# v prepared and loaded one block earlier, per-pair sums in another PSUM tile, squares on GpSimd, uneven block distances

## The chip, the cores and the metric

The kernel runs on one core of a Trainium2 chip. A core has a matrix engine (TensorE, PE in the profile) that writes to PSUM, three engines for element-wise work (VectorE as DVE, ScalarE as ACT, GpSimd as POOL), a queue engine that issues transfers (SyncE as SP), and 16 DMA engines. Each engine takes its own instructions in order; semaphores tie them together. The metric is the device time of one execution in microseconds, and lower is better.

## The reference

The program is attention with a sigmoid in place of a softmax, and a two-layer network behind it. Eight batches of 448 tokens, twelve heads of width 64, a model width of 768 and a hidden width of 2048:

```python
def _attn_ref(q, k, v):                      # (8, 12, 448, 64)
    S = q.shape[2]
    scale = 1.0 / np.sqrt(q.shape[-1])
    scores = scale * np.matmul(q, k.transpose(0, 1, 3, 2)) - np.log(S)
    attn = 1.0 / (1.0 + np.exp(-scores))
    return np.matmul(attn, v).astype(np.float32)

def _moe_ref(x, w_in, w_out):                # (3584, 768), (768, 2048), (2048, 768)
    h = x @ w_in
    g = h - np.tanh(h)
    return (g @ w_out).astype(np.float32)
```

## The kernel before

**Precision.** Most products are taken in float16 with each operand split into a high and a low half, three matmuls for one (high by high, high by low, low by high). A power-of-two scale goes with each split; it comes from sums of squares, which are summed over partitions by a small matmul against ones (`pbn` for q, k and v of a pair of heads, `nm` for x of a batch). The weights arrive in HBM as float64 and are converted on the chip during the first batch (`rawo` is a piece of `w_out` as it comes in, `stb` its converted form, `wl` the matmul over its squares).

**Stages.** Batch 0 takes its attention alone (`attention32`, in float32), while `w_in` is loaded and converted. After that the kernel alternates for each batch between `moe1` (x by `w_in`, 288 matmuls, PSUM tiles `ph`) and `moe2` (g by `w_out`, three groups of 128 tokens with 96 matmuls each into the two PSUM tiles of tag `mm`, and a last 64 tokens as `por`). The attention of the next batch is put into `moe2` in blocks. A group of tokens is counted in 16 steps of six `po` matmuls; the step numbers at which a block is put in are the tables `BLOCKS0` (batch 0), `BLOCKS1` (batch 1) and `BLOCKS` (later ones). A group ends at steps 16, 32 and 48: there ACT copies one half of its sum out of PSUM (L905, `o`), DVE the other (L906). The next group needs the same two PSUM tiles.

**Blocks.** `stream` takes two pairs of heads (128 columns each), g and h = g + 1, in four blocks, here called A, B, C and D. Each computes score tiles `sc` on PE, the sigmoid `a` of them on ACT (L394) and its two halves `ahl` (high on ACT L400, low on DVE L401).

- A: scores of g, chunks 0 and 1; then the products with v that are still owed (`do_av`), which closes the pair h before: ACT copies its result out as x (L430), squares it (`x2`, L439), and POOL adds the squares up (L448). Then the sums of squares of v for the next pairs (`norm_v`, two `sqn<-vn` on ACT, L317).
- B: scores of g, chunk 2 and the shared rest; sums of squares of k and q of g + 3. At steps 16, 32 and 48.
- C: the scales of g + 2 and g + 3 (`pbn` on PE, `tn` on ACT L330, small DVE instructions), scores of h, all products with v for g (closes g, with x and its square), the two halves `w` of k and q of g + 2, each of which goes through a transposing DMA to become K and Q.
- D: scores of h, chunk 2, k and q of g + 3 in the same way, and before the change the halves of v (`prep_v`, L369 and L370, `vhl`) of g + 2 and g + 3, and behind them the loads of v for g + 4 and g + 5 (`load_v`, into the two buffers `vn` that `prep_v` has just read).

In steady batches a batch starts with D at step 8, then A 12, B 16, C 20, D 24, A 28, B 32, C 36, D 40, A 44, B 48, C 52. `batch_scales` (`nm`) follows the last A by 3 steps.

**Order.** PE, ACT, DVE and POOL follow the order in which the program is written. SP's order, all loads and transposing DMAs, is made by the framework's scheduler. In batch 1 (whose attention runs in `moe2` of batch 0) q by k is split but v stays in float32: `early` is true there, so the products with v are spread over all four blocks and `pbn` uses a tile of the score tag `sc` (two buffers); later it uses the tag `av`.

Of the kernel before, what the change touches and what calls it, by code (L numbers as in the profile page):

```python
# [10 lines left out]
F32 = mybir.dt.float32  # L11
# [3 lines left out]
AF = mybir.ActivationFunctionType  # L15
ALU = mybir.AluOpType
# [3 lines left out]
P = 128  # L20
# [14 lines left out]
class Builder:  # L35
# [4 lines left out]
    SPLIT = 16, 0.78  # L40
    CONV = 0.95

    BLOCKS = (8, 12, 16, 20, 24, 28, 32, 36, 40, 44, 48, 52)
    TAIL = (1, 2, 3, 4, 5)
    ALONE = 9
    BLOCKS0 = (2, 5, 8, 12, 16, 20, 24, 31, 38)
    BLOCKS1 = (4, 7, 10, 13, 16, 20, 24, 28, 32, 36, 40, 44, 48, 52)

    TP = 8
    SHIFT = 4  # L50
# [268 lines left out]
    def scales(self, ss, where):  # L319


        nc = self.nc
        n = ss.shape[1] // 2
        if where == "sc":
            pb = self.ps.tile([P, 2, 512], F32, name="pbn", tag="sc", bufs=2)[:, 0, : 2 * n]
        else:
            pb = self.ps.tile([P, 512], F32, name="pbn", tag=where, bufs=1)[:, : 2 * n]
        nc.tensor.matmul(pb, self.onesf, ss, start=True, stop=True)
        t = self.sm.tile([P, 3, 2], F32, name="tn")
        nc.scalar.activation(  # L330
            t[:, :n].rearrange("p n i -> p (n i)"), pb, AF.Relu, bias=self.tiny, scale=2.1
        )
        u = self.sm.tile([P, 3], F32, name="un")
        nc.vector.tensor_tensor(u[:, :n], t[:, :n, 0], t[:, :n, 1], op=ALU.max)
        y = self.pow2(u[:, :n], n, "n")
        i = self.sm.tile([P, 3], F32, name="in")
        nc.vector.tensor_scalar(i[:, :n], y, 2.0**49, None, op0=ALU.mult)
        s = self.sm.tile([P, 3], F32, name="sn", bufs=3)
        nc.vector.reciprocal(s[:, :n], i[:, :n])
        r = self.sm.tile([P, 2], F32, name="rn", bufs=3)  # L340
        nc.vector.scalar_tensor_tensor(
            r[:, 0:1], i[:, 0:1], 1.0 / math.sqrt(D), i[:, 1:2], op0=ALU.mult, op1=ALU.mult
        )
        if n == 3:
            nc.vector.tensor_scalar(r[:, 1:2], y[:, 2:3], 2.0**49 / A_SCALE, None, op0=ALU.mult)
        return s, r
# [87 lines left out]
    def add_squares(self, j, x):  # L434

        nc = self.nc
        last = j == self.NP - 1
        x2 = self.xp.tile([P, self.S], BF16 if last else F32, name="x2", tag="x2", bufs=2)
        nc.scalar.activation(x2, x, AF.Square)  # L439
        if j == 0:  # L440
            self.x2 = x2
        elif last:
            self.x2b = self.x2, x2
        else:
            out = self.x2
            if j == self.NP - 2:
                out = self.xp.tile([P, self.S], BF16, name="x2b", tag="x2b", bufs=1)
            nc.gpsimd.tensor_tensor(out, self.x2, x2, op=ALU.add)  # L448
            self.x2 = out

    def stream(self):

        NP = self.NP
        G = (self.B - 1) * NP
        at = lambda g: (1 + g // NP, g % NP)
        splits = lambda g: at(g)[0] >= self.AV32
        qk, vn, sc, K, Q, vv, accs = {}, {}, {}, {}, {}, {}, {}  # L460

        def load(g):
            if g < G and g not in qk:
                qk[g] = self.load_qk(*at(g))

        def load_v(g):
            if g < G and splits(g):
                vn[g] = self.load_v(*at(g), self.nat, "vn", 2)

        def sums(g):  # L470
            ss = self.sums[g // 2 % 2]
            return ss if splits(g) else ss[:, :4]

        def norms(g):
            if g < G:
                for n, t in enumerate(qk[g]):
                    self.norm(t, sums(g)[:, 2 * n + g % 2 : 2 * n + g % 2 + 1])

        def norm_v(g):
            if g in vn:  # L480
                self.norm(vn[g], sums(g)[:, 4 + g % 2 : 5 + g % 2])

        def scales(g, where):
            if g < G:
                sc[g] = sc[g + 1] = self.scales(sums(g), where)

        def parts_k(g):
            if g < G:
                K[g] = self.parts(qk[g][0], sc[g][0][:, 0:1], "K", not splits(g) and g not in (2, 3))

        def parts_q(g):
            if g < G:
                Q[g] = self.parts(qk[g][1], sc[g][0][:, 1:2], "Q", True)
                qk.pop(g)

        def prep_v(g):
            if g >= G:
                return
            if splits(g):
                vv[g] = self.prep_v(vn.pop(g), sc[g][0])  # L500
            else:
                vv[g] = self.load_v(*at(g), self.att, "vhl", 3)[:, None]

        load(0)
        load(1)
        yield 0, False
        norms(0)
        norms(1)
        yield 0, False
        scales(0, "tr")  # L510
        parts_k(0)
        yield 450, False
        parts_q(0)
        load(2)
        yield 450, False
        parts_k(1)
        yield 450, False
        parts_q(1)
        load(3)
        yield 450, False  # L520
        norms(2)
        yield 0, False
        todo = []

        def open_acc(g):
            tag = "tr" if g % 2 else "av"
            accs[g] = self.ps.tile([P, 512], F32, name="acc", tag=tag, bufs=1)
            if g % NP == 0:
                self.xs = []

        def close_acc(g):
            iv = sc[g][1][:, 1:2] if splits(g) else None
            self.xs.append(self.evac_x(g % NP, accs.pop(g), iv))
            if g % 2:
                vv.pop(g - 1)
                vv.pop(g)
            for d in (sc, K, Q):
                d.pop(g)

        def do_av():  # L540
            for g, c, A in todo:
                odd = g % 2
                if c == QT:
                    open_acc(g + 1)
                    self.av([accs[g], accs[g + 1]], vv[g], A, c, odd)
                    close_acc(g)
                    continue
                if c == 0 and not odd:
                    open_acc(g)
                self.av([accs[g]], vv[g], A, c, odd)  # L550
                if c == QT - 1 and odd:
                    close_acc(g)
            todo.clear()

        def units(g, cs, between=lambda: None):

            pss = []
            for c in cs:
                n = 2 if c == QT else 1
                pss.append(self.scores([K[g + i] for i in range(n)], [Q[g + i] for i in range(n)], c))  # L560
            aa = [self.weigh(pss[0], sc[g][1][:, 0:1])]
            between()
            aa += [self.weigh(ps, sc[g][1][:, 0:1]) for ps in pss[1:]]
            return aa

        def keep(g, cs, aa):
            if splits(g):
                aa = [self.split_a(a) for a in aa]
            todo.extend((g, c, a) for c, a in zip(cs, aa))

        for g in range(0, G, 2):
            h = g + 1
            early = not splits(g)

            aa = units(g, (0, 1))
            do_av()
            if g == 0:
                prep_v(0)
                prep_v(1)
            keep(g, (0, 1), aa)  # L580
            load(g + 3)
            norm_v(g + 2)
            norm_v(g + 3)
            yield 2750, True

            aa = units(g, (2, QT))
            if early:
                do_av()
            norms(g + 3)
            keep(g, (2, QT), aa)  # L590
            yield 2750, True

            scales(g + 2, "sc" if early else "av")
            aa = units(h, (0, 1), lambda: parts_k(g + 2))
            do_av()
            keep(h, (0, 1), aa)
            parts_q(g + 2)
            load(g + 4)
            yield 2750, True

            aa = units(h, (2,), lambda: parts_k(g + 3))
            if early:
                do_av()
            keep(h, (2,), aa)
            parts_q(g + 3)
            prep_v(g + 2)
            prep_v(g + 3)
            load_v(g + 4)
            load_v(g + 5)
            norms(g + 4)  # L610
            yield 2750, True
        do_av()
        yield 1150, True
# [349 lines left out]
    def first(self, rest):  # L963
# [16 lines left out]
        next(rest)  # L980
        assert n + len(self.BLOCKS0) + len(self.BLOCKS1) == 4 * self.NP + len(self.BLOCKS) - self.ALONE
        split = self.split_w_in()
# [85 lines left out]
```

## Time and profile before

Three runs took 1281.15, 1287.76 and 1290.39 us. The profiled execution:

| | |
|---|---|
| median of three runs | 1287.76 us |
| profiled execution, its own time | 1281.98 us |
| its span | 1279.7 us |
| PE busy | 1190.1 us, 93% of the span |
| DVE, ACT, POOL busy | 908.4, 902.2, 37.9 us |
| one `moe1` (590.5 to 645.2 us) | 54.7 us, PE busy in all of it |
| `moe2` of batch 0 (153.5 to 282 us) | 128.5 us, PE busy 100.8 |
| `moe2` of batch 2 (496 to 590.5 us) | 94.5 us, PE busy 86.6 |

The page counts a matmul from its issue to its modelled end, and they overlap; 24 `po` matmuls take 4.07 us at the full clock, so 0.17 us each. What counts is where PE is idle, and the clock it is granted: 512 ns of idle time at the end of a group of tokens, with nothing between, is what the last batch shows; the batches with attention in them show more. In a row of the timeline the first two numbers are start and length in us, "xN" is a number of equal instructions merged into a row, and the bracket at its end says how long the engine had stood idle and which instruction ended that. A row of the waits reads: who, for whom, us in total, times, longest.

### The profile page before, as it was taken

The page shows a single profiled execution, that of the slowest core. Times are in us where ns is not written, and L with a number is a line of the kernel's source. Part 1 is how long each engine was busy: PE and PEld are TensorE (multiplying, and loading weights), DVE is VectorE, ACT ScalarE, POOL GpSimd, SP SyncE. Part 2 cuts the span into 40 slices and gives each one's busy share as a digit, 9 for nine tenths or more (in the row PEclk, how much of TensorE's full clock was granted, in tenths as well). Part 3 has the DMA queues.
Part 4 walks back from the last instruction along what each step waited for, and adds up shares of the span by engine and source line. Part 5 has one row for each costly group of instructions (what it writes and reads, how often), then busy time and mean ns, then how long its engine had stood idle before and what let it go on. Part 6 is the DMA issues. An engine that isn't in the chain of part 4 may idle for free.

```text
span 1279.7 us, 19703 instructions
## 1 busy us (share of the span) xinstructions
PE 1190.1 (93%) x7633; PEld 618.1 (48%) x7633; DVE 908.4 (71%) x1376; ACT 902.2 (70%) x1262; POOL 37.9 (3%) x38
## 2 busy tenths in 40 slices
PE   9899877699989999989999999999998999999998
PEld 3244323255445555445544555445554555455555
DVE  5899976678946689457975779556984689646940
ACT  6867785767877588766877768776877768763830
POOL 0100000000000000100000000000000000000000
PEclk9999999799999999999999999999999999999999
DMA  9963367120054400542024310353015410310000
GB/s 248 262 177 93 66 169 178 44 58 3 1 92 97 93 10 14 102 92 55 1 56 85 85 36 1 75 114 73 1 37 104 85 36 1 64 35 19 1 13 32
DMA packets 225678, 89.77 MB, mean 70 GB/s; under 512 B 213936, under 2 KB 215728, under 8 KB 225584
## 3 DMA queue, kind: packets, MB, share of 16 engines
q1 hardware_dynamic: 224656, 88.28, 30.5%
q8 instruction: 60, 0.98, 0.3%
q10 hardware_dynamic: 928, 0.23, 0.1%
q14 instruction: 34, 0.28, 0.1%
HBM read 58.20 MB, written 11.01 MB: 54 GB/s over the span
## 4 chain that ended last, share of the span: by engine, by line
PE 55%; DVE 13%; ACT 13%; DMA 9%; issue 6%; SPq 4%; DVEq 0%; ACTq 0%
PE ph L761 29%; PE po L876 12%; PE por L914 5%; PE acc L414 5%; DMA qn<-q 3%; PE sc L383 3%; ACT a L394 3%; DMA Q<-w 2%; SPq L298 2%; DVE ahl L401 2%; DMA rawo<-moe_w_out 1%; ACT sqn L317 1%; DVE m L835 1%; ACT ahl L400 1%; DVE m L849 1%
## 5 line engine op out<-in xcount | busy, mean ns | idle before, releaser
L876 PE MATMUL po<-wo,g 128*128 128x384 f16 x2304 | 402.6, 332 | 30.7 <-ACT o L905 28.8
L761 PE MATMUL ph<-xhl,wi 128*128 128x448 f16 x2016 | 382.6, 352 | 0.0
L876 PEld LDWEIGHTS <-g 128*128 128x128 f16 x2304 | 223.6, 99 | 212.7 <-issue 75.9
L761 PEld LDWEIGHTS <-wi 128*128 128x128 f16 x2016 | 196.7, 98 | 185.0 <-issue 2.1
L401 DVE SCALAR_TENSOR_TENSOR ahl<-a,ahl 128x896 f16<-128x896 f32 x126 | 137.7, 1127 | 178.9 <-ACT ahl L400 178.9
L394 ACT ACTIVATE a<-sc,nls,rn 128x896 f32<-128x896 f32 x147 | 154.2, 1089 | 24.7 <-PE sc L383 20.8
L831 ACT ACTIVATE u<-ph,ih 128x896 f32<-128x896 f32 x64 | 64.4, 1006 | 90.6 <-PE ph L761 85.9
L383 PE MATMUL sc<-Q,K 64*128 64x448 f16 x1008 | 104.3, 361 | 21.0 <-ACT tn L330 8.8
L400 ACT ACTIVATE ahl<-a 128x896 f16<-128x896 f32 x126 | 113.1, 939 | 0.6
L835 DVE SCALAR_TENSOR_TENSOR m<-ph,ihk,u 128x896 f32<-128x896 f32 x64 | 73.4, 1147 | 39.7 <-ACT th L833 39.4
L745 ACT ACTIVATE g<-m,Sg 128x896 f16<-128x896 f32 x64 | 66.6, 1041 | 39.2 <-DVE m L849 33.7
L414 PE MATMUL acc<-ahl,vhl 128*64 128x448 f16 (+1 forms) x864 | 82.1, 360 | 1.1 <-ACT tn L330 1.1
L849 DVE COPY_PREDICATED m<-u,th 128x896 f32<-128x896 uint32 x64 | 77.3, 1207 | 7.3 <-ACT u L831 0.5
L746 DVE SCALAR_TENSOR_TENSOR g<-m,Sg,g 128x896 f16<-128x896 f32 x64 | 73.4, 1147 | 6.8 <-ACT g L745 6.8
L846 DVE SCALAR_TENSOR_TENSOR m<-q,m 128x896 f32<-128x896 f32 x64 | 69.9, 1093 | 11.6 <-ACT q L845 3.9
L383 PEld LDWEIGHTS <-K 64*128 64x128 f16 x1008 | 36.9, 98 | 80.9 <-issue 58.8
L791 PE MATMUL ph<-x,wi 128*128 128x448 f32 x192 | 75.1, 540 | 0.2 <-DVE x L426 0.2
L836 DVE SCALAR_TENSOR_TENSOR th<-ph,ih,th 128x896 f32<-128x896 f32 x64 | 73.3, 1145 | 0.0
L848 ACT ACTIVATE u<-u,b 128x896 f32<-128x896 f32 x64 | 66.7, 1043 | 7.3 <-DVE m L835 5.4
L914 PE MATMUL por<-wo,g 128*64 128x384 f16 x768 | 64.9, 327 | 6.0 <-ACT o L905 6.0
L842 DVE SCALAR_TENSOR_TENSOR m<-q,m 128x896 f32<-128x896 f32 x64 | 69.6, 1088 | 0.0
L841 ACT ACTIVATE q<-u,b 128x896 f32<-128x896 f32 x64 | 65.8, 1029 | 0.0
(132 smaller groups left out, 1134.9 us busy)
## 6 DMA issues: line engine op xcount, KB each, us to landing
raw<-moe_w_in SPq DMA_DIRECT2D x24, 512.0 KB, 5.3
rawo<-moe_w_out SPq DMA_DIRECT2D x32, 384.0 KB, 4.1
kn<-k SPq DMA_DIRECT2D x96, 112.0 KB, 3.0
qn<-q SPq DMA_DIRECT2D x94, 112.0 KB, 3.0
vn<-v SPq DMA_DIRECT2D x96, 96.0 KB, 2.7
out<-o SPq DMA_DIRECT2D x21, 384.0 KB, 2.3
vn<-v SPq DMA_DIRECT2D x48, 32.0 KB, 2.5
out<-orem SPq DMA_DIRECT2D x16, 96.0 KB, 2.2
```

The source lines that it names most:

```text
L383: self.nc.tensor.matmul(ps[i * m : (i + 1) * m, h, : self.S], K[i][r, w, c * P : c * P + m], Q[i][r, x, :], start=(n == 0), stop=(n == len ...
L394: self.nc.scalar.activation(a[:, 0], ps[:, :, : self.S], AF.Sigmoid, bias=self.nls, scale=scale)
L400: nc.scalar.activation(A[:, 0], a[:, 0], AF.Copy, scale=A_SCALE)
L401: nc.vector.scalar_tensor_tensor(A[:, 1], a[:, 0], A_SCALE, A[:, 0], op0=ALU.mult, op1=ALU.subtract)
L414: self.nc.tensor.matmul(acc[i][h * D : (h + 1) * D, : self.S], v[k, w, 2 * QT + h if half else h * QT + c], A[k, x, h], start=(n == 0 and ...
L746: nc.vector.scalar_tensor_tensor(g[:, 1], m, Sg, g[:, 0], op0=ALU.mult, op1=ALU.subtract)
L761: nc.tensor.matmul(ph[:, e, :S], self.wi[:, c * self.NB + k, part, e * P : (e + 1) * P], xhl[c][:, x, :], start=(i == 0), stop=(i == 3 * s ...
L791: nc.tensor.matmul(ph[:, e, :S], self.where("in", c)[:, f * P : (f + 1) * P], xs[c], start=(c == 0), stop=(c == self.NC - 1),)
L835: V.scalar_tensor_tensor(m, ps, ihk, u, op0=ALU.mult, op1=ALU.mult)
L849: V.copy_predicated(m, u.bitcast(U32), th)
L876: nc.tensor.matmul(po[i][:, :H], gs[f // 2][:, x, f % 2, tk * P : (tk + 1) * P], self.wo[:, i * self.NF + f, w], start=(f == 0 and n == 0) ...
L914: nc.tensor.matmul(po[e * D : (e + 1) * D, :H], gs[f // 2][:, x, f % 2, nm:S], self.wo[:, e * self.NF + f, w], start=(f == 0 and n == 0), ...
```

## The change

Five edits go together. `prep_v` and `load_v` move from block D to block C, so the halves of v and the next loads of v stand one block sooner. `pbn` of the early pairs leaves the score tiles: it uses `mm` for g = 0 and `av` after that, and `early` now holds for g = 0 alone, so that the products with v of g = 2 and g = 4 are taken in A and C only. The squares of x go from ACT to POOL, but for the first and the last of a batch. Blocks at steps 12, 28 and 44 come at 11, 27 and 43 (all of them A); and `nm`, which hangs on the last, comes a step sooner too.

```diff
-    BLOCKS = (8, 12, 16, 20, 24, 28, 32, 36, 40, 44, 48, 52)
+    BLOCKS = (8, 11, 16, 20, 24, 27, 32, 36, 40, 43, 48, 52)
-    BLOCKS1 = (4, 7, 10, 13, 16, 20, 24, 28, 32, 36, 40, 44, 48, 52)
+    BLOCKS1 = (4, 7, 10, 13, 16, 20, 24, 27, 32, 36, 40, 43, 48, 52)
...
-        if where == "sc":
-            pb = self.ps.tile([P, 2, 512], F32, name="pbn", tag="sc", bufs=2)[:, 0, : 2 * n]
-        else:
-            pb = self.ps.tile([P, 512], F32, name="pbn", tag=where, bufs=1)[:, : 2 * n]
+        pb = self.ps.tile([P, 512], F32, name="pbn", tag=where, bufs=2 if where == "mm" else 1)[:, : 2 * n]
...
-        nc.scalar.activation(x2, x, AF.Square)
+        if last or j == 0:
+            nc.scalar.activation(x2, x, AF.Square)
+        else:
+            nc.gpsimd.tensor_tensor(x2, x, x, op=ALU.mult)
...
-            early = not splits(g)
+            early = g == 0
...
-            scales(g + 2, "sc" if early else "av")
+            scales(g + 2, "mm" if early else "av")
             aa = units(h, (0, 1), lambda: parts_k(g + 2))
             do_av()
+            prep_v(g + 2)
             keep(h, (0, 1), aa)
             parts_q(g + 2)
+            prep_v(g + 3)
             load(g + 4)
+            load_v(g + 4)
+            load_v(g + 5)
             yield 2750, True
...
             parts_q(g + 3)
-            prep_v(g + 2)
-            prep_v(g + 3)
-            load_v(g + 4)
-            load_v(g + 5)
             norms(g + 4)
```

What it does to the order is shown at three places. Line numbers behind L324 are lower by 3 in the changed kernel (L370 becomes L367, L401 becomes L398, L359 becomes L356).

The first is blocks C and D of a pair in `moe2` of batch 1, on DVE. In the names `w` is the pair of halves of k (`kn`) or q (`qn`), `sn` the scales, `vhl` those of v. Before:

```order
L357 SCALAR_TENSOR_TENSOR w<-kn,sn,w 112x512
L401 SCALAR_TENSOR_TENSOR ahl<-a_3092,ahl 128x896
L401 SCALAR_TENSOR_TENSOR ahl<-a_3099,ahl 128x896
L357 SCALAR_TENSOR_TENSOR w<-qn,sn,w 112x512
L356 TENSOR_SCALAR w<-kn,sn 112x512
L357 SCALAR_TENSOR_TENSOR w<-kn,sn,w 112x512
L401 SCALAR_TENSOR_TENSOR ahl<-a_3179,ahl 128x896
L357 SCALAR_TENSOR_TENSOR w<-qn,sn,w 112x512
L369 TENSOR_SCALAR vhl<-vn,sn 128x512
L370 SCALAR_TENSOR_TENSOR vhl<-vn,sn,vhl 128x512
L369 TENSOR_SCALAR vhl<-vn,sn 128x384
L370 SCALAR_TENSOR_TENSOR vhl<-vn,sn,vhl 128x384
```

The same place after the change:

```order
L354 SCALAR_TENSOR_TENSOR w<-kn,sn,w 112x512
L366 TENSOR_SCALAR vhl<-vn,sn 128x512
L367 SCALAR_TENSOR_TENSOR vhl<-vn,sn,vhl 128x512
L398 SCALAR_TENSOR_TENSOR ahl<-a_3092,ahl 128x896
L398 SCALAR_TENSOR_TENSOR ahl<-a_3099,ahl 128x896
L354 SCALAR_TENSOR_TENSOR w<-qn,sn,w 112x512
L366 TENSOR_SCALAR vhl<-vn,sn 128x384
L367 SCALAR_TENSOR_TENSOR vhl<-vn,sn,vhl 128x384
L353 TENSOR_SCALAR w<-kn,sn 112x512
L354 SCALAR_TENSOR_TENSOR w<-kn,sn,w 112x512
L398 SCALAR_TENSOR_TENSOR ahl<-a_3193,ahl 128x896
L354 SCALAR_TENSOR_TENSOR w<-qn,sn,w 112x512
```

The first v of the pair now stands ahead of C's two `ahl`, the second behind C's half of q; block D is four instructions shorter.

SP in `moe2` of batch 1, the pair whose block C stands at step 20 (K_3403 and Q_3453 are of g + 2, the next K and Q of g + 3). Before:

```order
L359 DMA_TRANSPOSE K_3403<-w_3400 128x8x112
L287 DMA kn_3455<-k 112x4x64 x2
L359 DMA_TRANSPOSE Q_3453<-w_3450 128x8x112
L287 DMA qn_3458<-q 112x4x64 x2
L359 DMA_TRANSPOSE K_3497<-w_3494 128x8x112
L287 DMA kn_3596<-k 112x4x64 x2
L359 DMA_TRANSPOSE Q_3505<-w_3502 128x8x112
L287 DMA qn_3599<-q 112x4x64
L298 DMA vn_3513<-v 128x3x64 x2
L302 DMA vn_3513<-v 64x2x64 x2
L298 DMA vn_3518<-v 128x3x64 x2
L287 DMA qn_3599<-q 112x4x64
```

The same place after the change:

```order
L356 DMA_TRANSPOSE K_3403<-w_3400 128x8x112
L287 DMA kn_3461<-k 112x4x64 x2
L298 DMA vn_3467<-v 128x3x64 x2
L302 DMA vn_3467<-v 64x2x64 x2
L356 DMA_TRANSPOSE Q_3456<-w_3453 128x8x112
L287 DMA qn_3464<-q 112x4x64 x2
L298 DMA vn_3472<-v 128x3x64 x2
L356 DMA_TRANSPOSE K_3511<-w_3508 128x8x112
L287 DMA kn_3590<-k 112x4x64
L356 DMA_TRANSPOSE Q_3519<-w_3516 128x8x112
L287 DMA kn_3590<-k 112x4x64
L287 DMA qn_3593<-q 112x4x64 x2
```

The six loads of v stood behind the last Q of the pair; four of them now stand ahead of the first Q, two ahead of the second K, and none is left in front of the next pair's q.

SP again, in `moe2` of batch 0, around the last pieces of `w_out` (`rawo`). Before:

```order
L359 DMA_TRANSPOSE Q_1658<-w_1655 128x8x112
L287 DMA qn_1663<-q 112x4x64 x2
L131 DMA rawo_1693<-moe_w_out 128x384
L131 DMA rawo_1707<-moe_w_out 128x384
L131 DMA rawo_1721<-moe_w_out 128x384
L298 DMA vn_1751<-v 128x3x64 x2
L131 DMA rawo_1778<-moe_w_out 128x384
L359 DMA_TRANSPOSE K_1735<-w_1732 128x8x112
L359 DMA_TRANSPOSE Q_1744<-w_1741 128x8x112
L131 DMA rawo_1792<-moe_w_out 128x384
```

The same place after the change:

```order
L356 DMA_TRANSPOSE Q_1663<-w_1660 128x8x112
L287 DMA kn_1668<-k 112x4x64 x2
L287 DMA qn_1671<-q 112x4x64 x2
L131 DMA rawo_1709<-moe_w_out 128x384
L131 DMA rawo_1723<-moe_w_out 128x384
L131 DMA rawo_1737<-moe_w_out 128x384
L131 DMA rawo_1774<-moe_w_out 128x384
L131 DMA rawo_1788<-moe_w_out 128x384
L356 DMA_TRANSPOSE K_1751<-w_1748 128x8x112
L356 DMA_TRANSPOSE Q_1756<-w_1753 128x8x112
```

The last piece of `w_out` stood behind the K and Q of block D, and now stands ahead of them; a load of k came ahead of the first of the five pieces.

On PE nothing but the places change: 18 in place of 24 `po` matmuls lie between D and A, 30 in place of 24 between A and B, and in batch 1's pairs g = 2 and g = 4 the products with v of blocks B and D are taken in C and A. ACT loses 32 squares and keeps its order otherwise; POOL has each square right ahead of the sum that takes it.

More of the change, by code (lines that the diff above doesn't have):

```diff
@@ L572, in stream @@
             h = g + 1
-            early = not splits(g)
+            early = g == 0
             aa = units(g, (0, 1))
             do_av()
-            if g == 0:
+            if early:
                 prep_v(0)
```

## The prediction, made before the run

> **What bounds it now.** I read the busy shares first, then who PE waits for by engine, then the timeline around the largest wait, and last the granted clock there.
>
> ```profile
> PE 1190.1 (93%) x7633; PEld 618.1 (48%) x7633; DVE 908.4 (71%) x1376; ACT 902.2 (70%) x1262; POOL 37.9 (3%) x38
> ```
>
> PE has 90 us in which it is not busy, and POOL is almost free. The waits (us in total, times, longest):
>
> ```profile
> PE po L876 <- ACT o L905: 28.8, 13, 4.1
> PE por L914 <- ACT o L905: 6.0, 7, 1.8
> PE sc L383 <- DVE m L690: 4.5, 5, 1.5
> PE sc L383 <- DMA Q<-w: 3.0, 2, 1.7
> ACT sqn L317 <- DMA vn<-v: 33.7, 30, 2.9
> ```
>
> The largest wait of PE, for the copies L905 that free its PSUM tiles at a group's end, has a partner: ACT waits as long for loads of v. The timeline of one group's end in batch 2's `moe2` ties them together:
>
> ```profile
> 512.49 1.77 ACT L400 ACTIVATE ahl<-a 128x896 f16<-128x896 f32 x2
> ...
> 514.70 1.69 SPq L298 DMA_DIRECT2D vn<-v  x2
> ...
> 515.72 0.60 DVE L906 TENSOR_SCALAR o<-po,iK 128x384 f32<-128x384 f32 x1
> ...
> 517.17 0.63 ACT L317 ACTIVATE sqn<-vn 128x512 bf16<-128x512 f32 x1 [2.90 <-DMA vn<-v]
> ...
> 518.74 0.56 ACT L905 ACTIVATE o<-po,iK 128x384 f32<-128x384 f32 x1
> 519.35 5.63 PE L876 MATMUL po<-wo,g 128*128 128x384 f16 x24 [2.72 <-ACT o L905]
> ```
>
> DVE copies its half as soon as the group is done (515.72). ACT copies its half 3.02 us later, because its queue holds A's `sqn` ahead of L905, and the v that it squares was issued only at 514.70. PE stands 2.72 us. Then 24 `po` take 5.63 us; elsewhere 4.06:
>
> ```profile
> 519.35:524.98 5.63, 5.63 (x26) 3.10 (x25) 1.61 (x2) 4.82 (x8) 0.00 (x0) 0.71 0.19 72
> ```
>
> This row of the windows (the granted clock is the third number from the end) shows a clock of 0.71 where the page has 0.9 or more in most slices. Six stalls are followed by such slow matmuls; the first, the last, and a shorter stall without:
>
> ```profile
> 372.54 5.65 PE L876 MATMUL po<-wo,g 128*128 128x384 f16 x24 [4.07 <-ACT o L905]
> ...
> 697.73 4.06 PE L876 MATMUL po<-wo,g 128*128 128x384 f16 x24 [2.36 <-ACT o L905]
> ...
> 988.93 5.74 PE L876 MATMUL po<-wo,g 128*128 128x384 f16 x24 [2.71 <-ACT o L905]
> ```
>
> So a stall of about 2.6 us or more is charged twice: its length, and some 1.65 us (5.63 to 5.74, less 4.06) of slow clock.
>
> **The change, part by part.** *v in C.* The loads of v are issued in C instead of D, four steps (4.07 us below) and D's own scores sooner, some 6 to 8 us, so `sqn` no longer waits. Without the wait ACT ends L400 at 512.49 + 1.77 = 514.26 and two `sqn` (2 x 0.63) at 515.5, before the group ends at 515.72. What stays is the copy itself, as in the last batch, which has no blocks:
>
> ```profile
> PE po L876 <- ACT o L905: 1.0, 2, 0.5
> PE por L914 <- ACT o L905: 0.6, 1, 0.6
> ```
>
> But in batches 1 to 6 block B's scores lie between two groups and cover that 0.5. So 28.8 - 1.0 = 27.8 of `po` goes, and of `por` 6.0 - 0.6 - 0.5 = 4.9 (0.5 being batch 6's last 64 tokens, which have no block): **-32.7**. With stalls of 2.6 us gone, six slow stretches go: 6 x 1.65 = **-9.9**. Moving A from 12 to 11 helps the same wait once more (ACT is there one step, 4.06 / 4 = 1.02 us, sooner), so I allow a residue for q's squares only: they stand in B ahead of L905, and q's loads now stand behind the four v loads on SP. Such a wait is there today:
>
> ```profile
> 688.95 0.63 ACT L317 ACTIVATE sqn<-qn 112x512 bf16<-112x512 f32 x1 [1.14 <-DMA qn<-q]
> ```
>
> Bounds 0 and 1.14 at each of 16 group ends (11 `po`, 5 `por`); nearer to 0, since most `qn` are in time now: 0.2 x 16 = **+3**.
>
> *`nm` a step sooner.* It removes the wait for L690, 1.02 us sooner against a longest wait of 1.5; I take the 4.5 with half a us around it, **-5** (ends -2.5 and -5).
>
> *The price: A asks for Q sooner.* The scores of A need the Q that C of the same pair made. Batch 2, the pair before:
>
> ```profile
> 529.62 0.58 ACT L439 ACTIVATE x<-x 128x448 f32<-128x448 f32 x1
> 530.27 1.13 POOL L448 TENSOR_TENSOR x<-x,x 128x448 f32<-128x448 f32 x1 [16.43 <-ACT x L439]
> 531.07 2.29 DVE L401 SCALAR_TENSOR_TENSOR ahl<-a,ahl 128x896 f16<-128x896 f32 x2 [3.54 <-ACT ahl L400]
> ...
> 533.47 4.07 PE L876 MATMUL po<-wo,g 128*128 128x384 f16 x24
> 534.05 1.22 SPq L359 DMA_TRANSPOSE Q<-w  x1
> 537.09 0.72 ACT L354 ACTIVATE w<-qn,sn 112x512 f16<-112x512 f32 x1 [1.42 <-DMA Q<-w]
> 537.48 1.31 PE L383 MATMUL sc<-Q,K 64*128 64x448 f16 x12
> ```
>
> Q is there at 537.09 (ACT, held by the same transfer, goes on then), and A starts at 537.48: 0.39 us of slack. At step 11 PE comes 1.02 sooner, 0.63 too soon. The square of 0.58 leaves ACT's path to Q. But POOL now issues two operations of 1.13 in place of one, and DVE, which makes the low halves that C's products need before Q's turn, doesn't run beside them:
>
> ```profile
> 53.86 1.14 POOL L448 TENSOR_TENSOR x<-x,x 128x448 f32<-128x448 f32 x1 [7.13 <-ACT x L439]
> 54.01 1.54 DVE L152 SCALAR_TENSOR_TENSOR sta<-raw,sta 128x512 uint32<-128x512 uint32 x1
> ...
> 56.65 0.69 DVE L152 SCALAR_TENSOR_TENSOR sta<-raw,sta 128x512 uint32<-128x512 uint32 x1
> ```
>
> A form that takes 0.69 alone takes 1.54 beside POOL, and ends 0.55 us after POOL does. So: 0.63 - 0.58 + 1.13 = 1.18 a time. Ends: 0.05 (POOL adds nothing) and 1.76 (ACT's gain reaches Q not at all). I take 1.2, since DVE in C goes straight on to `ahl`. Of the A blocks that moved and are followed by a new Q there are 11 (27 and 43 in batches 1 to 5, 27 in batch 6): **+13** (0.6 to 19). That PE can wait for Q so is in the trace: 3.0 in two, above. Whoever is queued behind A's scores on PE, the `po` matmuls, waits along.
>
> *`prep_v` in C* puts 1.2 us on DVE ahead of `ahl`. It fits into the 3.54 that DVE stands idle there (row 531.07): 0 (if ACT came sooner than DVE ends, up to 1.2 at 12 places). Four v loads now stand ahead of Q on SP (ns: least, median, most):
>
> ```profile
> L298 SPq DMA_DIRECT2D vn<-v x96: 368/487/2180, 1.7 to 1104.3; - x96
> L302 SPq DMA_DIRECT2D vn<-v x48: 599/629/1305, 2.8 to 1103.0; - x48
> ```
>
> Two of each are 2 x 0.49 + 2 x 0.63 = 2.2 us; K is issued near 530, so they are done at 532.3, before Q's 534.05: 0. The K of g + 3 is moved behind two more, and is needed only in B: 0.
>
> *`moe2` of batch 0.* `pbn` for g = 4 leaves the score tiles, so that the wait for its `tn` moves:
>
> ```profile
> 207.10 0.43 SPq L131 DMA_DIRECT2D rawo<-moe_w_out  x1
> ...
> 213.76 0.57 SPq L131 DMA_DIRECT2D rawo<-moe_w_out  x1
> ...
> 217.94 0.57 ACT L146 ACTIVATE stb<-rawo 128x384 f32<-128x384 f32 x1 [3.98 <-DMA rawo<-moe_w_out]
> ...
> 222.93 1.72 PE L414 MATMUL acc<-a,vn 128*64 128x448 f32 x8
> ...
> 232.04 0.39 PE L328 MATMUL pbn<-ss,onesf 128*128 128x6 f32 x2 [3.38 <-ACT sqn L317]
> ...
> 240.41 0.25 ACT L330 ACTIVATE tn<-pbn,tiny 128x6 f32<-128x6 f32 x1
> 240.72 1.30 PE L383 MATMUL sc<-Q,K 64*128 64x448 f16 x6 [7.09 <-ACT tn L330]
> ```
>
> PE stands 7.09 us because scores need the tile that holds `pbn` until ACT's `tn`. After the change `acc` (tag `av`) needs that tile instead, a few matmuls later: the wait is moved, not removed. What can shrink it is ACT coming sooner: its wait of 3.98 for the last piece of `w_out` (issued at 213.76, and in the new order ahead of K and Q, so near 208) goes, for 0 to 4 us. Against that, more products with v are packed into A and C, in bursts of 8 in 1.72. I take **-3**, ends -6 and +2.
>
> *Squares in `attention32`* (batch 0): four go to POOL, each holds DVE up to 1.1 and spares ACT 0.58: **+1** (0 to +2).
>
> **The sum**: -32.7 - 9.9 + 3 - 5 + 13 - 3 + 1 = -33.6. The profiled execution took 1281.98, so 1248.4; it lies 5.8 below the median of the runs, 1287.76, from which the same sum gives 1254. I say 1250.
>
> **Rivals.** *The group ends keep half.* If SP's order still brings v or q late, the 16 ends keep some 0.8 more each (+13) and two or three of six slow stretches stay (+4): with the residue near 1270. For it: `sqn` of q waits 1.14 today. Against: v moves by 6 us or more, and the longest wait is 2.9. *It goes better.* A never waits (end 0.6 for 13) and batch 0 gives 6 or more: 1250 - 12.4 - 3 is about 1235, with the residue zero 1231. *The slow clock stays.* The clock falls for another cause than the stalls: +9.9, so 1260. In the rows six drops follow the six longest stalls and none a shorter one of 2.36. The Trainium skill ("TensorE: Matmul & The Clock Gate", Part 1) has the clock fall only after an idle window of about 3.4 us. By it five of the six stalls were too short, and their slow stretches might stay; the trace doesn't bear this out, with a drop after 2.71.
>
> *Slower.* A's wait for Q is longer than worked out, and each becomes a stall that also lowers the clock. Place: Q on SP, in order behind the v loads. Two and two of these by the longest rows above are 7.0 us from 530: Q issued at 537 and not 534.05, so the wait is 1.2 + 2.9, about 4, and with 1.65 of slow clock 5.7 at 11 places, 62 in place of 13: near 1297. It decides from a wait of 2.6: 11 x (2.6 + 1.65) = 47, which is all that is gained. Against: medians give 2.2 us, and the issues would have to be slow each time.
>
> **How the numbers follow.** My forecast (1237 to 1264) 0.60; half kept (1264 to 1275, or a little more) 0.17; better (1228 to 1237) 0.12; the slow clock stays (1255 to 1265) 0.05; slower 0.06. The range 1232 to 1272 leaves out about half of "better", a third of "half kept" and "slower": under 0.2. One per cent, about what a measurement of this kernel tells from no change, is 12.9 us: faster is below 1274.9. That holds for the forecast, better, the clock, and most of half kept, in all 0.86; same 0.10 (the rest of it, and a milder form of "slower"); slower 0.04.
>
> **What would show it.** Right: `sqn` waiting for v is near zero; `po` waiting for L905 falls from 28.8 to a few us; every 24 `po` take 4.07; scores waiting for L690 are gone; a new wait of scores for Q, about 13 us in 11; POOL runs some 70 operations, with longer `ahl` on DVE beside them; ACT takes the last `stb` near 214. Wrong: if the waits for Q have lengths of 2.6 or more with slow `po` behind; if `sqn` of q takes over the wait of v; if L905 is still late without any wait ahead of it, ACT is busier in A than I think.

## The result and the profile after

| | before | changed |
|---|---|---|
| median, four runs each | 1289.08 us (1281.15 to 1290.48) | 1248.98 us (1248.06 to 1250.92) |
| ratio | | 0.970, 95% interval 0.966 to 0.975 |
| profiled execution: time, span | 1281.98, 1279.7 | 1250.92, 1249.1 |

The forecast was 1250, with 1232 to 1272 around it. By stages (start of the first `ph` or `po` matmul of one stage to that of the next, us, from the timeline of PE; `only_v` and `v_step_qv` are experiments below):

| stage | before | changed | `only_v` | `v_step_qv` |
|---|---|---|---|---|
| attention of batch 0 | 67.1 | 69.8 | 70.4 | 67.5 |
| `moe1` of batch 0 | 101.4 | 102.9 | 101.4 | 103.1 |
| `moe2` of batch 0 | 113.7 | 116.3 | 112.7 | 109.6 |
| `moe2` of batch 1 | 104.4 | 98.0 | 97.8 | 93.6 |
| `moe2` of batch 2 | 94.9 | 85.3 | 85.3 | 83.5 |
| `moe2` of batch 3 | 91.7 | 85.2 | 84.4 | 83.5 |
| `moe2` of batch 4 | 92.5 | 85.5 | 85.0 | 83.5 |
| `moe2` of batch 5 | 91.6 | 85.5 | 85.0 | 83.5 |
| `moe2` of batch 6 | 79.8 | 77.9 | 77.2 | 77.2 |
| each later `moe1`; end | 54.5; 61.3 | 54.5; 61.3 | 54.5; 61.3 | 54.5; 61.3 |

The changed kernel gains 37.4 us in `moe2` of batches 1 to 6 and gives back 6.8 in batch 0. (The 128.5 us that stand ahead of the prediction for `moe2` of batch 0 begin at 153.5, with blocks of attention in front of the first `po` at 168.5; the table counts from that `po`.) The page's line of busy times, and the waits of PE by engine and line (us in total, times, longest):

```profile
PE 1183.5 (95%) x7633; PEld 612.2 (49%) x7633; DVE 932.9 (75%) x1376; ACT 884.6 (71%) x1230; POOL 87.3 (7%) x70
```

```profile
PE wl L179 <- DVE stb L152: 13.3, 9, 5.6
PE sc L380 <- DMA Q<-w: 12.3, 13, 2.1
PE acc L411 <- ACT tn L327: 9.4, 3, 7.1
...
PE por L914 <- ACT o L905: 1.1, 2, 0.6
PE po L876 <- ACT o L905: 1.0, 2, 0.5
...
PE po L876 <- DVE o L906: 0.6, 1, 0.6
PE sc L380 <- DVE m L690: 0.3, 1, 0.3
```

The two lines for L905, 34.8 us before, hold 2.1. New near the top stands the wait of scores for Q; the wait for `tn` has gone over from scores to the products with v (`acc`). ACT's wait for v is in no row; q's is, as before. The same group's end in batch 2 as the prediction showed, in the timeline of the changed kernel:

```profile
513.20 3.09 DVE L398 SCALAR_TENSOR_TENSOR ahl<-a,ahl 128x896 f16<-128x896 f32 x2 [3.14 <-ACT ahl L397]
513.48 1.87 POOL L448 TENSOR_TENSOR x<-x,x 128x448 f32<-128x448 f32 x1
513.90 0.62 ACT L317 ACTIVATE sqn<-vn 128x512 bf16<-128x512 f32 x1
...
514.51 0.52 ACT L317 ACTIVATE sqn<-vn 128x384 bf16<-128x384 f32 x1
...
515.50 0.58 ACT L905 ACTIVATE o<-po,iK 128x384 f32<-128x384 f32 x1 [0.37 <-PE po L876]
...
515.55 1.43 PE L380 MATMUL sc<-Q,K 64*128 64x448 f16 x18
516.21 0.60 DVE L906 TENSOR_SCALAR o<-po,iK 128x384 f32<-128x384 f32 x1
```

ACT's `sqn` have no bracket: v is there. ACT now waits for PE at L905 (0.37), and its copy ends under the scores of B. DVE's copy L906 has become the later one: it stands behind two `ahl` that take 3.09 us beside POOL, and ends at 516.81, just before B's scores do.

The price, at the same place as in the prediction:

```profile
525.68 0.93 POOL L439 TENSOR_TENSOR x<-x 128x448 f32<-128x448 f32 x1 [10.34 <-ACT x L427]
526.41 3.10 DVE L398 SCALAR_TENSOR_TENSOR ahl<-a,ahl 128x896 f16<-128x896 f32 x2 [0.62 <-ACT ahl L397]
526.69 1.86 POOL L448 TENSOR_TENSOR x<-x,x 128x448 f32<-128x448 f32 x1
...
528.19 1.39 SPq L302 DMA_DIRECT2D vn<-v  x2
...
529.42 0.74 DVE L354 SCALAR_TENSOR_TENSOR w<-qn,sn,w 112x512 f16<-112x512 f32 x1
...
530.19 1.26 SPq L356 DMA_TRANSPOSE Q<-w  x1
...
533.31 1.31 PE L380 MATMUL sc<-Q,K 64*128 64x448 f16 x12 [0.74 <-DMA Q<-w]
```

Q is issued the moment DVE has its low half (529.42 + 0.74 = 530.16); SP's loads of v were done 0.6 us before (528.19 + 1.39 = 529.58). PE then stands 0.74 us.

### The profile page after: what moved, and what is told of

Same layout as the page of the kernel before. It is cut to its first block, busy times and chain, and to the rows that moved or that the text cites. A ratio compares the mean times of both kernels' runs of the same rounds, so it can differ in the third digit from the quotient of the medians.

```text
span 1249.1 us, 19741 instructions
## 1 busy us (share of the span) xinstructions
PE 1183.5 (95%) x7633; PEld 612.2 (49%) x7633; DVE 932.9 (75%) x1376; ACT 884.6 (71%) x1230; POOL 87.3 (7%) x70
## 3 DMA queue, kind: packets, MB, share of 16 engines
q1 hardware_dynamic: 224656, 88.28, 31.1%
## 4 chain that ended last, share of the span: by engine, by line
PE 65%; DVE 13%; ACT 10%; issue 6%; DMA 5%; SPq 1%; DVEq 0%; ACTq 0%
PE ph L761 30%; PE po L876 17%; PE acc L411 6%; PE por L914 5%; PE sc L380 5%; DMA Q<-w 3%; DVE ahl L398 3%; ACT ahl L397 3%; ACT a L391 2%; ACT sqn L317 2%; DVE sta L152 1%; DMA rawo<-moe_w_out 1%; DVE w L354 1%; DVE m L835 1%; DVE m L846 1%
## 5 line engine op out<-in xcount | busy, mean ns | idle before, releaser
L876 PE MATMUL po<-wo,g 128*128 128x384 f16 x2304 | 393.4, 327 | 4.6 <-DVE wo L219 2.0
L876 PEld LDWEIGHTS <-g 128*128 128x128 f16 x2304 | 219.5, 98 | 179.5 <-issue 39.0
L398 DVE SCALAR_TENSOR_TENSOR ahl<-a,ahl 128x896 f16<-128x896 f32 x126 | 156.9, 1279 | 137.3 <-ACT ahl L397 137.3
L380 PE MATMUL sc<-Q,K 64*128 64x448 f16 x1008 | 104.6, 362 | 17.3 <-DMA Q<-w 12.3
L439 POOL TENSOR_TENSOR x<-x 128x448 f32<-128x448 f32 x32 | 30.9, 965 | 1023.3 <-ACT x L427 788.5
L846 DVE SCALAR_TENSOR_TENSOR m<-q,m 128x896 f32<-128x896 f32 x64 | 69.9, 1092 | 10.9 <-ACT q L845 3.9
```

What stands on the lines that cost most here:

```text
L380: self.nc.tensor.matmul(ps[i * m : (i + 1) * m, h, : self.S], K[i][r, w, c * P : c * P + m], Q[i][r, x, :], start=(n == 0), stop=(n == len ...
L398: nc.vector.scalar_tensor_tensor(A[:, 1], a[:, 0], A_SCALE, A[:, 0], op0=ALU.mult, op1=ALU.subtract)
L846: V.scalar_tensor_tensor(m, q2, C2, m, op0=ALU.add, op1=ALU.mult)
L876: nc.tensor.matmul(po[i][:, :H], gs[f // 2][:, x, f % 2, tk * P : (tk + 1) * P], self.wo[:, i * self.NF + f, w], start=(f == 0 and n == 0) ...
```

## The experiments

A ratio is to the kernel before on the same chip, with its 95% interval. Each experiment undoes one part of the change, does one part alone, or goes on from it.

**1. `undo_v`: v back in D.**

```diff
-            prep_v(g + 2)
             keep(h, (0, 1), aa)
             parts_q(g + 2)
-            prep_v(g + 3)
             load(g + 4)
-            load_v(g + 4)
-            load_v(g + 5)
...
             parts_q(g + 3)
+            prep_v(g + 2)
+            prep_v(g + 3)
+            load_v(g + 4)
+            load_v(g + 5)
```

> The changed kernel, with the halves and the loads of v back in block D. Theory (ACT waits for a late v with L905 behind it): ACT's sqn waits for v again, some 30 us in all; PE's wait for L905 at the ends of groups returns from 1.0 + 1.1 to 25 to 33 us, with some stalls over 2.5 us and 24 po of 5.6 us behind them; scores waiting for Q stay or shrink (four v loads fewer ahead of Q). Time 1280 to 1292. Rival (A a step sooner and the squares off ACT made the group ends whole): L905 stays under 8 us, time 1250 to 1258.

1294.81 us (1289.59 to 1299.35), ratio 1.003 (1.000 to 1.005). The waits of this kernel:

```profile
PE po L876 <- ACT o L905: 22.5, 12, 3.5
...
PE sc L380 <- DMA Q<-w: 10.3, 13, 1.3
...
PE por L914 <- ACT o L905: 7.2, 7, 1.8
```

```profile
ACT sqn L317 <- DMA vn<-v: 43.1, 29, 3.7
```

All of the gain goes with this part, and the rival falls. ACT's wait for v is even longer than before (43.1 against 33.7): an earlier ACT only waits longer for the same load. The time lies 3 us above the range given: of what the other four parts cost, batch 0 is 6.0 us longer than in the kernel before (288.2 against 282.2) and scores wait 10.3 us for Q in place of 3.0, while L690 gives back 3.7 (0.8 in place of 4.5).

**2. `undo_step`: A back at 12, 28 and 44.**

```diff
-    BLOCKS = (8, 11, 16, 20, 24, 27, 32, 36, 40, 43, 48, 52)
+    BLOCKS = (8, 12, 16, 20, 24, 28, 32, 36, 40, 44, 48, 52)
-    BLOCKS1 = (4, 7, 10, 13, 16, 20, 24, 27, 32, 36, 40, 43, 48, 52)
+    BLOCKS1 = (4, 7, 10, 13, 16, 20, 24, 28, 32, 36, 40, 44, 48, 52)
```

> The changed kernel, with the blocks A back at steps 12, 28 and 44. Theory (A at 27 and 43 asks 1.02 us too soon for Q, and v alone mends the group ends): scores waiting for Q fall from 12.3 us to under 3; scores waiting for L690 return to 4 or 5; L905 stays under 4 us, since ACT has no wait ahead of it. Time 1243 to 1249, so 0 to 6 below the changed kernel. Rival (the sooner A is what lets ACT reach L905 in time): L905 returns with 0.5 to 1 us at each of 16 group ends, 8 to 16 us, time 1252 to 1262.

1249.31 us (1248.19 to 1250.81), ratio 0.968 (0.966 to 0.970), the same as the changed kernel and just above the theory's range.

```profile
PE sc L380 <- DVE m L690: 4.5, 5, 1.1
PE po L876 <- DVE o L906: 4.3, 6, 1.1
...
PE sc L380 <- DMA Q<-w: 3.2, 2, 2.0
```

The waits for Q and for L690 went as the theory said: 9.1 saved, 4.2 given back. L905 is not late, so the rival falls. What neither named is the third line: with A a step later, DVE's copy L906 is the one that is late, 4.3 us where it had 0.6, since the `ahl` ahead of it are held up by POOL (in batch 2 the pair takes 3.10 us from 537.25, L906 starts at 540.27, and PE waits 0.57). The sooner A pays for itself and no more.

**3. `undo_sq`: squares of x back on ACT.**

```diff
-        if last or j == 0:
-            nc.scalar.activation(x2, x, AF.Square)
-        else:
-            nc.gpsimd.tensor_tensor(x2, x, x, op=ALU.mult)
+        nc.scalar.activation(x2, x, AF.Square)
```

> The changed kernel, with all squares of x back on ACT. Theory (two POOL operations hold up the low halves that Q waits for): scores waiting for Q fall from 12.3 to 5 or 6 us (0.55 less each), the attention of batch 0 is 2 to 3 us shorter (69.8 to about 67 us), L905 stays under 4; time 1240 to 1245. Rival (POOL costs nothing; Q is late because A comes sooner and v's loads are ahead of it on SP): waits for Q stay at 10 us or more, or grow by ACT's 0.58 each to 18; time 1249 to 1256.

1246.14 us (1243.55 to 1247.30), ratio 0.965 (0.963 to 0.968). The waits for Q stay: 10.9 us in 13. This was the rival's number, and the theory's "5 or 6" is a miss; the time lies between the two ranges. It was also worked out wrongly: 0.55 was taken from the whole wait, though 0.63 of it comes from the sooner A alone. The place of the prediction, here:

```profile
523.27 2.29 DVE L398 SCALAR_TENSOR_TENSOR ahl<-a,ahl 128x896 f16<-128x896 f32 x2 [1.29 <-ACT ahl L397]
...
529.37 1.31 PE L380 MATMUL sc<-Q,K 64*128 64x448 f16 x12 [0.59 <-DMA Q<-w]
```

The pair of `ahl` takes 2.29 where it took 3.10, but DVE starts it later, since ACT's square of 0.58 is ahead of ACT's `ahl` again. The wait is 0.59, not 0.74: the squares add 0.15 at this A.

Most of the time fell elsewhere. In `moe1` of batch 0 a matmul waits for the last x but one, which DVE copies (L423): 1.6 us in each of the seven profiles with squares on POOL, 0.2 in each of the seven without. (L426 is the same line in the kernel before.) Changed kernel, then before:

```profile
75.45 1.02 PE L791 MATMUL ph<-x,wi 128*128 128x448 f32 x2 [1.60 <-DVE x L423]
```

```profile
71.36 1.02 PE L791 MATMUL ph<-x,wi 128*128 128x448 f32 x2 [0.25 <-DVE x L426]
```

`moe1` of batch 0 takes 99.9 us here and 102.9 in the changed kernel. This wait is 1.4 of the 3.0, and a half-clock window nearly all the rest: in the changed kernel PE is idle for 1.85 us of the stretch from 74.39 to 77.80, and from 77.80 to 81.21 the granted clock is 0.50. That second part doesn't come each time: `undo_early` has the wait without the window. The time of the whole attention of batch 0 doesn't follow: 67.1 and 68.1 us in two of the kernels without squares on POOL, 70.4 in a third.

**4. `undo_early`: small sums back in the score tiles, products with v over four blocks in batch 1's pairs.**

```diff
-        pb = self.ps.tile([P, 512], F32, name="pbn", tag=where, bufs=2 if where == "mm" else 1)[:, : 2 * n]
+        if where == "sc":
+            pb = self.ps.tile([P, 2, 512], F32, name="pbn", tag="sc", bufs=2)[:, 0, : 2 * n]
+        else:
+            pb = self.ps.tile([P, 512], F32, name="pbn", tag=where, bufs=1)[:, : 2 * n]
...
-            early = g == 0
+            early = not splits(g)
...
-            if early:
+            if g == 0:
...
-            scales(g + 2, "mm" if early else "av")
+            scales(g + 2, "sc" if early else "av")
```

> The changed kernel, with the sums of squares of batch 1's pairs back in the score tiles and their products with v spread over all four blocks. Theory (the wait for tn was only moved from scores to the products with v): one wait of some 7 us for tn stands before scores again, and moe2 of batch 0 takes 113 to 117 us as with the change (116.3); nothing moves after it; time 1246 to 1251. Rival (this part made batch 0 longer): moe2 of batch 0 about 113.5 and time 1246 or less; the other rival, that it is what shortens batch 0: over 119 us there, time over 1252.

1247.44 us (1246.88 to 1248.76), ratio 0.966 (0.964 to 0.969). The wait of some 7 us for `tn` is back before scores, as long as before:

```profile
243.52 1.30 PE L383 MATMUL sc<-Q,K 64*128 64x448 f16 x6 [7.62 <-ACT tn L330]
```

and in the changed kernel it stands before the products with v:

```profile
246.92 5.77 PE L411 MATMUL acc<-a,vn 128*64 128x448 f32 x20 [7.05 <-ACT tn L327]
```

So it was moved and not removed. But `moe2` of batch 0 is 112.4 us here, just under the range of the theory and against the 116.3 of the changed kernel: the first rival is right that this part made it longer, though its time, 1246 or less, was not reached. Over all profiles of this study it is 116.0 to 117.4 in the six with this part, and 109.6 to 113.7 in the eight without. The two traces differ already between the first blocks B and C of `moe2`. The changed kernel:

```profile
193.92 0.33 PE L179 MATMUL wl<-stb,onesb 128*128 128x384 bf16 x1 [1.82 <-DVE stb L152]
...
199.46 0.39 PE L325 MATMUL pbn<-ss,onesf 128*128 128x4 f32 x2 [1.24 <-ACT sqn L317]
```

and this one:

```profile
190.22 2.41 PE L414 MATMUL acc<-a,vn 128*64 128x448 f32 x8
...
196.42 0.29 PE L328 MATMUL pbn<-ss,onesf 128*128 128x4 f32 x2
```

With its products with v taken away from block B, PE reaches the next `wl` before the piece of `w_out` for it is converted, and C's `pbn` comes 9.87 us after B's first score (at 189.59). With the eight products in B PE waits for neither, and it is 8.46 (from 187.96). It is 9.5 to 9.9 in the six profiles with this part, 8.2 to 8.5 in the eight without.

**5. `control`: the changed kernel again.**

> The changed kernel itself, on the chip of this series. Both theories: 1247 to 1252; scores waiting for Q 11 to 13 us, batch 0 (to the start of batch 1's moe1) 287 to 291 us in its profile. It shows how far batch 0 and its half-clock windows (12 in the first profile, 8 in the kernel before) repeat.

1250.37 us (1244.55 to 1252.36), ratio 0.966 (0.964 to 0.969). Waits for Q 11.5 in 13; batch 0 takes 288.4 us (69.0, 103.0 and 116.4), with 12 half-clock windows as in the first profile. What batch 0 loses repeats.

**6. `only_v`: the kernel before with v in C.** The diff is that of 1, the other way.

> The kernel before, with the halves and loads of v in block C and nothing else. Theory (v alone mends the group ends; the other parts bring 5 for L690, cost 9 in waits for Q and 6 in batch 0): ACT's wait for v under 2 us, L905 under 5, waits for Q under 4, L690 4 to 5, DVE's copy L906 late by some 4 as without the step; batch 0 282 to 284 us; time 1240 to 1247. Rival (the parts need each other: with A at 12 and the square on ACT, ACT is late at L905 even without the wait): L905 10 us or more, time 1252 to 1262.

1243.92 us (1241.70 to 1244.22), ratio 0.961 (0.960 to 0.963).

```profile
PE po L876 <- ACT o L905: 3.9, 7, 1.5
PE sc L383 <- DVE m L690: 3.8, 5, 1.0
...
PE sc L383 <- DMA Q<-w: 3.0, 2, 1.7
```

One of five edits brings more than all five. The waits are where the theory had them (L690 a little lower), but DVE's copy is not late (0.2 us): with A at 12 it is in `undo_step`, 4.3, where POOL squares. Batch 0 takes 284.5 us (70.4, 101.4, 112.7), half a microsecond above what was expected. The parts don't need each other.

**7. `v_step`: v in C and the sooner A, nothing else.**

> The kernel before, with v in block C and the blocks A at 11, 27 and 43: the changed kernel without its squares on GpSimd and without its new place for the small sums. Theory (those two parts lengthen batch 0 by 3 us each and bring nothing after it): batch 0 281 to 285 us, waits for Q 9 to 11 us, no L905; time 1241 to 1246. Rival (the lengths of batch 0 are chance between executions): batch 0 286 us or more and time 1247 to 1251.

1243.36 us (1241.62 to 1244.95), ratio 0.962 (0.960 to 0.963), as `only_v`. Waits for Q 9.9, L905 2.8 of which 1.8 in batch 1; batch 0 takes 283.1 us, so its losses are not chance.

**8. `q_first`: the changed kernel with the halves of q ahead of the low halves of C's scores.**

```diff
             prep_v(g + 2)
-            keep(h, (0, 1), aa)
             parts_q(g + 2)
+            keep(h, (0, 1), aa)
             prep_v(g + 3)
```

> The changed kernel, with the halves of q of g + 2 made ahead of the low halves of block C's scores on ACT and DVE, not behind them. Theory (Q's issue waits for its low half w on DVE, which stands behind two ahl of 3.10 us; SP's loads of v are done before): Q is issued 2 to 3 us sooner, waits for Q fall from 12.3 to under 4 (those of batches 0 and the first of batch 1 may stay), no new wait of the products for ahl, since they are needed 7 steps later; time 1239 to 1243. Rival (SP in order, v's loads ahead of Q, sets Q): Q is issued less than 1 us sooner, waits for Q stay over 8 us, time 1246 to 1251.

1241.89 us (1241.44 to 1244.05), ratio 0.961 (0.959 to 0.963). Waits for Q fall to 4.8 in 10, not quite under 4. The time is the theory's, the mechanism only half: Q is issued 525.46 - 516.82 = 8.64 us after C's scores begin, 0.51 sooner than in the changed kernel (530.19 - 521.04 = 9.15), not 2 to 3.

```profile
516.82 1.31 PE L380 MATMUL sc<-Q,K 64*128 64x448 f16 x12
...
521.95 0.98 DVE L354 SCALAR_TENSOR_TENSOR w<-qn,sn,w 112x512 f16<-112x512 f32 x1 [0.39 <-ACT w L351]
...
523.97 1.38 SPq L302 DMA_DIRECT2D vn<-v  x2
525.46 1.26 SPq L356 DMA_TRANSPOSE Q<-w  x1
```

The low half is ready at 522.93, and Q goes out only behind the loads of v, done at 525.35. DVE set Q in the changed kernel, with SP 0.6 us behind it; take DVE away and SP sets it.

**9. `v_step_q`: `v_step` with the order of 8.**

> v in block C and the sooner A (squares and small sums as before the change), with the halves of q of g + 2 made ahead of the low halves of block C's scores. Theory (after that, SP's four v loads in front of Q are the last that Q waits for, and cost a rest of some 0.2 us a time): waits for Q 4 to 6 us in all, of which 3.0 in the two that the kernel before has; batch 0 281 to 285 us; time 1234 to 1239. Rival (DVE or ACT still set Q, and the saving came from elsewhere): waits for Q over 7, time 1240 to 1244.

1237.60 us (1236.39 to 1239.79), ratio 0.959 (0.956 to 0.962). Waits for Q 6.7 in 12, a little over the 4 to 6 expected; the two at 27 and 43 in batch 2 are 0.27 and 0.29. The time fits the theory.

**10. `v_step_qv`: the first `prep_v` behind the halves of q too.** SP's order, which the scheduler makes, then has Q ahead of every load of v.

```diff
-            prep_v(g + 2)
             parts_q(g + 2)
+            prep_v(g + 2)
             keep(h, (0, 1), aa)
             prep_v(g + 3)
```

> The kernel v_step_q with the first prep_v of block C behind the halves of q, so that SP issues Q ahead of all loads of v. Theory (SP's order sets Q in v_step_q): Q is issued 2 to 3 us sooner after C's scores than in the changed kernel, waits for Q at 27 and 43 are gone, 3 to 4 us left in all, v lands 1 to 2 us later and is still in time; time 0 to 4 below v_step_q. Rival (v's loads are on the edge: later, they bring ACT's wait and L905 back): sqn waits for v 5 us or more, L905 over 6, time 2 to 10 above v_step_q.

1231.08 us (1229.86 to 1234.03), ratio 0.954 (0.951 to 0.957): the fastest kernel of the study, some 18 us below the changed one and 6.5 below 9.

```profile
514.73 1.22 SPq L359 DMA_TRANSPOSE Q<-w  x1
...
517.23 0.97 SPq L298 DMA_DIRECT2D vn<-v  x2
518.24 1.95 SPq L302 DMA_DIRECT2D vn<-v  x2
```

```profile
PE sc L383 <- DMA Q<-w: 2.4, 2, 1.8
```

C's scores begin at 507.78 here, so Q is issued 6.95 us later, 2.2 sooner than in the changed kernel and 1.7 sooner than in 9 (519.27 - 510.63 = 8.64). No A at 27 or 43 waits for Q any more, v is still in time (no row of ACT's waits names it), and each steady `moe2` takes 83.5 us. It gained 6.5, more than the 0 to 4 expected.

**11. `only_step` and 12. `only_sq`: the kernel before with one of these parts.** The diffs are those of 2 and 3, the other way.

> The kernel before with the blocks A at 11, 27 and 43 and nothing else. Theory (ACT waits for v whatever the step of A): ACT's sqn waits for v 30 to 45 us, L905 of po 22 to 30 us in all, L690 under 1, waits for Q 5 to 10; ratio 0.995 to 1.005. Rival (the step helps the group ends by itself): L905 under 16, ratio 0.985 or less.

1291.11 us (1283.57 to 1297.71), ratio 1.000 (0.997 to 1.003). L905 29.1 in 13 for `po`, L690 0.2, waits for Q 9.6: as the theory had it.

> The kernel before with the squares of x on GpSimd and nothing else. Theory (they free 0.58 us of ACT a block where ACT waits for v anyway, and cost 1 to 2 us in batch 0's moe1): moe1 of batch 0 102.5 to 103 us (101.4 before), L905 within 3 us of 28.8, ratio 0.999 to 1.005. Rival (ACT's 0.58 comes through at the group ends): L905 22 or less, ratio 0.995 or less.

1295.90 us (1289.63 to 1302.70), ratio 1.005 (1.002 to 1.008). The ACT time that the squares free does not come through: ACT waits longer for v.

```profile
ACT sqn L317 <- DMA vn<-v: 49.4, 32, 4.2
```

```profile
PE po L879 <- ACT o L908: 33.3, 13, 3.9
```

(L908 is L905 of the other kernels.) The group ends became 4.5 us worse, not better; the theory said within 3. `moe1` of batch 0 took 104.3 us, above the 102.5 to 103 expected: 1.4 more for the wait of 1.6 seen in 3, and a third half-clock window, where the kernel before has two. Why ACT waits still longer for v stays open.

## Why the prediction was right, point by point

- *v in C, -32.7.* Measured: 28.8 + 6.0 became 1.0 + 1.1, so -32.7. `only_v` and `undo_v` show that this part does nearly all of it alone: 3.9 + 1.1 are left in `only_v`.
- *Six slow stretches, -9.9.* After the start of batch 1's `moe1` the clock records of the trace have 7 half-clock windows before and 1 after. All rows of 24 `po` from there on take 4.06 to 4.13 in the changed kernel. Right in size; the rule behind it, "a stall of about 2.6 us or more", was only near the truth (last section). Nor do the six drops follow the six longest stalls: the sixth longest, 2.57 at 1107.80, is followed by none, and one of 2.56 at 668.62 is.
- *Residue at the group ends, +3.* Nothing to speak of: 0.6 for L906, once. ACT still waits for q (6.8 us in 11, before 9.7 in 12), but at no group's end does PE wait for it.
- *`nm` sooner, -5.* 4.5 became 0.3, and the 0.7 for `nm` itself is gone: -4.9.
- *The price, +13.* 8.9 at the 11 places, 0.81 a time and not 1.18; over all waits for Q, 12.3 against 3.0. The mechanism held: without the squares 0.59 is left (`undo_sq`), for which the sum had 0.63. What was too large is POOL's part: it lengthens the pair of `ahl` by 3.10 - 2.29 = 0.81, not 1.13, and 0.58 of that comes back from ACT. SP's four loads, which the sum set at 0, were indeed hidden, but by 0.6 us and not by the 1.8 worked out: K (issued at 524.67) and the loads of k, 1.22 and 1.14 us, stand ahead of them in the same queue and were not counted; `q_first` and `v_step_qv` show it coming out as soon as DVE is mended.
- *`moe2` of batch 0, -3, and squares in the attention, +1.* This is the step that failed. The wait for `tn` was moved as said (7.09 to 7.05). But the hoped-for gain, ACT sooner at the last piece of `w_out`, did not come: ACT takes that piece 49.7 us into the stage, before 49.4. The stage became 2.6 us longer than before, and is 3.9 longer than in `undo_early`. The wait of 3.98 for the last piece went, and one of 6.63 for the first of the last five stands in front of it (5.94 before):

```profile
212.54 2.40 SPq L131 DMA_DIRECT2D rawo<-moe_w_out  x5
...
216.66 0.55 ACT L146 ACTIVATE stb<-rawo 128x384 f32<-128x384 f32 x1 [6.63 <-DMA rawo<-moe_w_out]
```

  All five are issued together at 212.54, 39.9 us into the stage. Before the change the first of them went out at 204.61, 36.1 us into it, and with `undo_early` at 209.56, 36.6 us into it; over all profiles it is 39.3 to 39.9 in the six with this part and 35.7 to 37.1 in the eight without. The wait itself doesn't tell (7.59 in `undo_early`, 8.33 in `only_v`). The prediction looked at the last piece alone, and set it near 208; it did not ask what the products with v had covered in block B. The pieces come behind block C, and C is later, in part for the reason shown in experiment 4. That this part of the change costs the stage 3 to 4 us is shown; the rest of the chain is not, nor which half of the part does it, the tile of `pbn` or the place of the products, since no run takes them apart.

  The 6.8 us of batch 0 are 2.7 of attention, 1.4 of `moe1` and 2.6 of `moe2`. In `moe1` three things add up: this part takes away a wait for `tn` of 1.4 (gone in all six profiles with it), the squares add 1.4 (experiment 3), and a third half-clock window adds 1.6 (`v_step_qv` has it with neither: 103.1 against 101.4). In `moe2` PE is idle for 1.4 us more and busy for 1.2 more, with 7 half-clock windows in place of 5. The attention's length varies by 3 us between kernels whose code doesn't differ there, so its 2.7 stay open.

So the sum, -33.6, met the measured -31.1 of the two profiled executions (1281.98 to 1250.92) partly because two misses cancel: the group ends and Q came out 7 better (3 + 4), batch 0 some 9 worse. Of the rivals, none came: the waits for Q stayed at 1.2 us or less but for one of 2.12 (in batch 1; it did lower the clock, once), and L905 did not keep its half.

## What to carry to other kernels

When an in-order engine waits for a load while holding work that frees another engine's buffer, move the load, not the work: one such edit was worth all the gain here, and freeing time on the waiting engine was worth nothing. Of a bundle, time each part alone: the other four together made the kernel 5 to 6 us slower than this one edit, and v and the sooner A alone, with the halves of q put first, come out 1.3 to 1.4% below the bundle. When a transfer is late, list everything that must end before its issue with the margin of each: the second in line (here SP's queue, 0.6 us behind DVE) is what the next edit will meet.

## What the runs showed of the hardware that was not expected

Whether a stall lowers the clock is not told by its length, but by how much of one window on a fixed grid it fills. Half-clock windows begin at multiples of 3.413 us from one another within a run. In the kernel before, a stall of 2.71 us ends at 988.93 and lowers the clock, and one of 2.57 that ends at 1107.80 doesn't. The windows view cut along that grid (us, PE busy, PEld, DVE, ACT, POOL, then the granted clock, DMA share and GB/s):

```profile
986.81:990.22 3.41, 1.29 (x8) 0.78 (x8) 0.00 (x0) 2.64 (x7) 0.00 (x0) 1.00 0.34 100
990.22:993.63 3.41, 3.41 (x13) 1.62 (x11) 0.69 (x1) 3.41 (x7) 0.00 (x0) 0.50 0.16 61
1102.86:1106.27 3.41, 2.37 (x25) 0.96 (x23) 2.41 (x3) 1.07 (x3) 0.00 (x0) 1.00 0.57 126
1106.27:1109.69 3.42, 1.89 (x12) 1.17 (x12) 0.00 (x0) 3.02 (x6) 0.00 (x0) 1.00 0.57 177
1109.69:1113.10 3.41, 3.41 (x28) 1.93 (x25) 1.29 (x2) 3.41 (x9) 0.00 (x0) 1.00 0.00 0
```

The first stall leaves PE 2.12 us idle in one window, and the next window runs at half the clock. The second is cut by a grid line into 1.04 and 1.53, and nothing follows. In six of these profiles (before, changed, `undo_v`, `undo_step`, `only_step`, `only_sq`) all 27 cases after the start of batch 1 in which a stall took 2.05 us or more of one window were followed by a half-clock window. Between 1.90 and 2.03 two of four were. Shorter ones were so only where they shared the window, or the stall, with more idle time. Counted by whole windows over all fourteen profiles, from the same start: 38 of the 38 with 2.05 us or more idle were followed, 8 of the 24 with 1.65 to 2.03, and of those with less only two, which ran at half the clock themselves. So some 60% of a window, idle, is enough, and half of one is sometimes. The Trainium skill ("TensorE: Matmul & The Clock Gate", Part 1) has the half clock come after at least one idle window of about 3.4 us; the length of the window agrees with 3.413, a whole window of idleness does not.
